# Zeroing a new batch's first column on VectorE, and reading the weighted sums behind the mask of the slot

## The chip, the cores and the metric

The kernel runs on one core of a Trainium2 chip. The metric is the device time of one execution in microseconds (us); the median of several runs is compared.

## What is computed

The reference is an attention that keeps only the 32 largest scores of each query, followed by a channel mix with a token shift. Shapes: 8 batches, 8 heads, 576 tokens, 64 columns per head; model width 512, hidden width 1024.

```python
scores = scale * np.matmul(q, k.transpose(0, 1, 3, 2))
kth = np.partition(scores, -top_k, axis=-1)[..., -top_k:-top_k + 1]
scores = np.where(scores >= kth, scores, -1000000000.0)
attn = np.exp(scores - np.max(scores, axis=-1, keepdims=True))
attn = attn / (np.sum(attn, axis=-1, keepdims=True) + 1e-09)
x = np.matmul(attn, v)                      # then (B, S, H * D)
x_prev = np.concatenate([np.zeros((B, 1, D)), x[:, :-1, :]], axis=1)
xk = mu_k * x + (1.0 - mu_k) * x_prev
xr = mu_r * x + (1.0 - mu_r) * x_prev
k = np.maximum(xk @ w_k, 0.0)
out = 1.0 / (1.0 + np.exp(-(xr @ w_r))) * (k * k @ w_v)
```

The first token of a batch has no token before it, so `x_prev` begins with a column of zeros.

## The kernel before

The attention is cut into 288 tiles of 128 queries. Two heads are worked on together; for each batch the program visits four pairs of heads with tiles 0 to 3 and then the same four pairs with tiles 4 to 8. The program is a pipeline of slots, written out in Python: in slot n the loop in `pipeline` issues one step each for several tiles that stand at different stages, in the order that the list `ORDER` (line 42) gives. Nothing reorders it afterwards; every engine runs its own instructions in exactly this order and waits on semaphores.

The steps that matter here, with the tile that each serves in slot n:

- `score` (tile n, L234 and L238): TensorE multiplies queries and keys into the PSUM tile `ps`.
- `keep` (tile n, L243): ScalarE copies `ps` to `sc` in SBUF.
- `c0` to `c6`, `best`, `drop`, `bounds` (tiles n-1 and n-2, L267 to L279): VectorE picks the largest scores of each piece of a row.
- `count` (tile n-2, L283) on ScalarE and `below` (L286) on GpSimd; `eighth` (L914) and `thr` (L291) on VectorE then find the threshold of tile n-3.
- `exp` (tile n-3, L294): ScalarE writes the exponentials into the PSUM tile `se`, of which there is one. `mask` (tile n-3, L297): VectorE multiplies `se` by the comparison with the threshold and writes `E`; its time includes a short reading of the row's sum.
- `turn` (tile n-4, L313): TensorE transposes `E`, ScalarE copies the result out as `et` (L314).
- `weigh` (tile n-5, L371 and L373): TensorE multiplies the transposed weights with the values.
- `place` (tile n-6, L379 or L384, in 96 of the slots, where a group of four tiles or the last single one is complete): VectorE multiplies these weighted sums by the inverse row sums `ri` and writes them to `xT`, the transposed rows of the batch. This is what the title calls reading the weighted sums; below it is the **place**.

The scores and the weighted sums lie in the same PSUM tile, side by side in the same two banks:

```python
scored = p("psS", 1, space=PSUM).tile([128, 2, 512], F32, name="ps")
g.ps = scored[:, :, :HS]
g.sums = scored[:, :, HS:HS + 128], scored[:, 0, HS + 128:HS + 192]
```

So the program has the next `score` on TensorE wait until the place has read the sums, and the place wait until `keep` has read the scores.

The channel mix runs in the same slots. Chunks of up to 256 tokens of finished rows are mixed (L403, L408, L413), split into a high and a low part (L427, L428) and multiplied with the weights (L432 to L434). This work comes in queues by engine (`L.soft`), from which a slot takes as much as a budget allows. `xT` has two buffers, one for each of two batches. Therefore, when the first place of a batch comes and the batch is the third or a later one, `L.force(g.read)` first issues all queued work up to the last reading of the rows, whatever the budget. Then `new_batch` takes the buffer and sets its first column to zero, 4 elements on each of 128 partitions (L690), on GpSimd. This happens eight times, at the first place of each batch. In the first 230 us VectorE, ScalarE and GpSimd also turn the weights of the channel mix, which come as 64-bit numbers, into pairs of 32-bit ones (L122 to L147).

Of the kernel before, what the change touches and what calls it, by code (L numbers as in the profile page):

```python
# [38 lines left out]
PACE, SHARE, PIECE, CAP, MOST = 4.60, 0.74, 1.52, 4.45, 2  # L39
END, HASTE = 36, 1.20  # L40
EXPS, EVAC = 3, (0, 'et')
ORDER = """exp norm score turn prep inv loads evac keep weigh sign best0 c0 drop0 c1 best1 c2 drop1 first c3 best2 c4 bounds eighth count et high below act late c5 norm2 early thr c6 second place mix mask dve pool weights""".split()


@with_exitstack
def topk_attention_channel_mix(ctx: ExitStack, tc: tile.TileContext, q, k, v, mu_k, mu_r, w_k, w_v, w_r, out):
    nc = tc.nc
# [639 lines left out]

    def new_batch(g):
        x = g.two.tile([128, HP, 1 + S], F32, name="xT")
        nc.gpsimd.memset(x[:, :, 0:1], 0.0)  # L690
        return x

    def pipeline(g):
# [91 lines left out]
        while n < total + 7 or "next" in state or L.busy():  # L785
# [96 lines left out]
            def ranks_(f, r):  # L882
                if C:
                    f(C, r)
# [40 lines left out]
            def place_():  # L925
                T = tiles.get(n - 6)
                if T and ends(T):
                    U = T.U
                    if U.P.b not in xT:
                        if state["start"] < (U.P.b - 1) * S:  # L930
                            save()
                        if U.P.b > 1:
                            L.force(g.read)
                        xT[U.P.b] = new_batch(g)
                    U.xT = xT[U.P.b]
                    place(U)
                    if U.P.hp == HP - 1 and T.i == U.P.part[-1]:
                        state["tokens"] = U.P.b * S + (S if T.i == 8 else 256)
                if V and V.i == V.P.part[-1] and V.P.hp == HP - 1:
                    o = slice(V.P.first, V.i + 1)  # L940
                    nc.vector.tensor_reduce(least[:, V.P.n // HP:V.P.n // HP + 1], V.P.group[:, :, 1:, o], axis=mybir.AxisListType.XYZ, op=OP.min)
# [5 lines left out]
            do.update({f"drop{r}": lambda r=r: ranks_(drop, r) for r in range(2)})  # L947
            for step in ORDER:
                if step in do:
# [24 lines left out]
    with tc.If(again > 0):  # L974
        with tc.For_i(0, B, 1) as b, ExitStack() as stack:
            g = Env()
            open_pools(stack, g, "_again")
            L = Direct()
            xT = new_batch(g)
            rows = out[bass.ds(b, 1)].rearrange("o s d -> (o s) d")  # L980
            for hp in range(HP):
# [56 lines left out]
```

## Time and profile before

| what | us |
|---|---|
| median of 3 runs (lowest, highest) | 1448.99 (1447.81, 1449.4) |
| the profiled execution | 1450.08 |
| its span, from the first to the last instruction | 1448.2 |

The profile is of one execution. Its trace says of every instruction when it began, how long it took, how long its engine stood idle before it and which instruction of another engine ended that idle time. "PE" is TensorE's matmuls, "PEld" its weight loads, "DVE" VectorE, "ACT" ScalarE, "POOL" GpSimd. A name such as `xT<-ps,ri` gives the tile written and the tiles read. The chain of waits is followed back from the last instruction to what released it at each step.

### The profile page before, as it was taken

Reading aid. Unit: us, or ns where it says so; the run is one execution under the profiler, and the core shown is the slowest. Engines: PE = TensorE matmul, PEld = TensorE weight load, DVE = VectorE, ACT = ScalarE, POOL = GpSimd, SP = SyncE. Lnnn points to the kernel's source line nnn. Section 1 sums busy time; section 2 is a strip of 40 time slices with the busy share of each in tenths; the row PEclk is TensorE's granted clock in tenths of the full one; section 3 lists DMA queues with packets and bytes.
Section 4 is the critical chain, followed back from the end, with each engine's and each line's share of the span. In section 5 each row is a group of like instructions: output and inputs, shape, how many; then the busy total and the mean of one; then the engine's idle time right before and its main releaser. Section 6 shows DMA issues by size and latency. Waiting matters only on the chain.

```text
span 1448.2 us, 32903 instructions
## 1 busy us (share of the span) xinstructions
PE 1289.6 (89%) x9909; PEld 971.8 (67%) x9909; DVE 1205.7 (83%) x6454; ACT 1160.8 (80%) x2662; POOL 968.2 (67%) x876
## 2 busy tenths in 40 slices
PE   5657767999989999898989999999999998999997
PEld 3444555676867676675767687777767676777786
DVE  6999899888888888888888988888888897889610
ACT  5677777898879888878879899888888887888741
POOL 3658886576656865656758776776676765667683
PEclk9886888999999999999999999999999999899999
DMA  4332232222121222112121222212221222111000
GB/s 98 82 91 75 55 88 70 57 48 57 45 64 39 59 60 60 41 44 62 44 60 40 52 59 57 47 50 62 54 58 41 49 64 65 33 45 42 20 16 21
DMA packets 243817, 78.79 MB, mean 54 GB/s; under 512 B 236464, under 2 KB 236464, under 8 KB 243632
## 3 DMA queue, kind: packets, MB, share of 16 engines
q1 hardware_dynamic: 243632, 76.61, 21.9%
q8 instruction: 82, 1.34, 0.4%
q14 instruction: 103, 0.84, 0.2%
HBM read 67.11 MB, written 9.44 MB: 53 GB/s over the span
## 4 chain that ended last, share of the span: by engine, by line
PE 59%; DVE 19%; ACT 13%; POOL 5%; issue 2%; DMA 1%; SPq 0%; ACTq 0%; DVEq 0%; POOLq 0%
PE ps L371 8%; PE ps L234 8%; PE pt L313 6%; PE ph L432 5%; PE ph L433 4%; PE ph L434 4%; PE pv L432 4%; PE pv L434 4%; PE pv L433 4%; DVE cand L267 3%; DVE E L297 3%; ACT sc L243 3%; ACT sg L283 2%; DVE top L914 2%; ACT xm L408 2%
## 5 line engine op out<-in xcount | busy, mean ns | idle before, releaser
L286 POOL TENSOR_TENSOR sg<-sc,sg 128x576 f32<-128x576 f32 x288 | 420.8, 1461 | 410.3 <-ACT sg L283 363.7
L267 DVE MAX8 cand<-sc 128x8 f32<-128x82 f32 (+1 forms) x2016 | 465.9, 231 | 4.5 <-ACT sc L243 3.7
L243 ACT ACTIVATE sc<-ps 128x576 f32<-128x576 f32 x288 | 186.3, 647 | 128.1 <-PE ps L234 104.6
L234 PE MATMUL ps<-K,qs 64*128 64x288 f32 x1024 | 206.4, 482 | 57.8 <-DVE xT L379 42.6
L283 ACT ACTIVATE sg<-sc,seen 128x576 f32<-128x576 f32 x288 | 222.1, 771 | 44.3 <-DVE seen L278 40.5
L914 DVE MAX8 top<-sg 128x8 f32<-128x576 f32 x288 | 216.6, 752 | 33.4 <-POOL sg L286 32.6
L297 DVE SCALAR_TENSOR_TENSOR E<-sc,seen,se 128x576 f32<-128x576 f32 x288 | 232.7, 808 | 0.9 <-DVE cand L267 0.6
L294 ACT ACTIVATE se<-sc,seen 128x576 f32<-128x576 f32 x288 | 213.8, 742 | 24.1 <-DVE E L297 23.7
L313 PEld LDWEIGHTS pt<-ident,E 128*128 128x128 f32 x1152 | 127.1, 146 | 152.6 <-issue 101.0
L313 PE MATMUL pt<-ident,E 128*128 128x128 f32 x1152 | 197.5, 297 | 32.6 <-DVE E L297 29.2
L371 PE MATMUL ps<-et,v_in 128*64 128x128 f32 (+1 forms) x2560 | 178.5, 286 | 27.4 <-ACT sc L243 26.4
L432 PE MATMUL ph<-xh,wk 128*128 128x256 f32 (+2 forms) x608 | 180.2, 296 | 1.1 <-ACT r L449 0.9
L371 PEld LDWEIGHTS ps<-et,v_in 128*64 128x64 f32 x2560 | 140.2, 147 | 59.6 <-ACT sc L243 51.6
L433 PE MATMUL ph<-xl,wk 128*128 128x256 f32 (+2 forms) x608 | 172.7, 284 | 8.3 <-POOL xl L428 8.3
L270 DVE MAX8 top<-cand 128x8 f32<-128x56 f32 x864 | 176.1, 204 | 0.1
L434 PE MATMUL ph<-xh,wk 128*128 128x256 f32 (+2 forms) x608 | 171.3, 282 | 0.0
L314 ACT ACTIVATE et<-pt 128x512 f32<-128x512 f32 x288 | 168.6, 585 | 1.5 <-PE pt L313 1.5
L234 PEld LDWEIGHTS ps<-K,qs 64*128 64x128 f32 x1024 | 81.9, 196 | 126.4 <-DVE xT L379 45.9
L432 PE MATMUL pv<-wv,hh 128*128 128x512 f32 (+1 forms) x296 | 126.3, 427 | 0.1
L433 PEld LDWEIGHTS ph<-xl,wk 128*128 128x128 f32 x608 | 116.6, 192 | 10.7 <-POOL xl L428 10.5
L432 PEld LDWEIGHTS ph<-xh,wk 128*128 128x128 f32 x608 | 116.4, 191 | 9.9 <-issue 6.2
L434 PE MATMUL pv<-wv,hl 128*128 128x512 f32 (+1 forms) x296 | 118.2, 399 | 2.8 <-POOL hl L453 2.7
(99 smaller groups left out, 2858.0 us busy)
## 6 DMA issues: line engine op xcount, KB each, us to landing
kt<-in_k SPq DMA_DIRECT2D x256, 72.0 KB, 2.3
q_near<-in_q SPq DMA_DIRECT2D x256, 64.0 KB, 2.2
v_in<-in_v SPq DMA_DIRECT2D x128, 128.0 KB, 2.5
out<-eb SPq DMA_DIRECT2D x35, 256.0 KB, 2.2
wst<-in_moe_w_k SPq DMA_DIRECT2D x8, 512.0 KB, 4.1
wst<-in_moe_w_v SPq DMA_DIRECT2D x8, 512.0 KB, 3.8
vr_in<-in_v SPq DMA_DIRECT2D x64, 32.0 KB, 2.4
wst<-in_moe_w_r SPq DMA_DIRECT2D x4, 512.0 KB, 4.0
```

Source lines behind the costliest of these rows:

```text
L234: nc.tensor.matmul(g.ps[:, e], lhsT=P.qs[j][h, c * 128:(c + 1) * 128], rhs=P.K[h, j], start=True, stop=True)
L243: nc.scalar.activation(T.sc.rearrange("p (e k) -> p e k", e=2), T.ps, AF.Copy)
L267: nc.vector.max(T.cand[:, 8 * i:8 * i + 8], T.sc[:, CUTS[i]:CUTS[i + 1]])
L283: nc.scalar.activation(T.side, T.sc, AF.Sign, bias=T.under, scale=-BELOW, accum_out=T.cnt)
L286: nc.gpsimd.tensor_mul(T.side, T.sc, T.side)
L297: nc.vector.scalar_tensor_tensor(T.e, T.sc, T.thr, g.pe, op0=OP.is_ge, op1=OP.mult, accum_out=T.rs)
L313: nc.tensor.transpose(pt[:, c, :], T.e[:, c * 128:(c + 1) * 128], ident)
L371: nc.tensor.matmul(pa[hs[j]], lhsT=P.v[:, j, c, :], rhs=ms[c][j], start=(c == 0), stop=False)
L432: nc.tensor.matmul(ps, lhsT=sh, rhs=mh, start=first, stop=False)
L433: nc.tensor.matmul(ps, lhsT=sh, rhs=ml, start=False, stop=False)
L434: nc.tensor.matmul(ps, lhsT=sl, rhs=mh, start=False, stop=last)
L914: nc.vector.max(M.top[:, 24:32], M.side)
```

## The change

Two things change. The memset of a new batch's first column goes from GpSimd to VectorE. And in `ORDER` the step `mask` stands ahead of `place`, which leaves `place` as VectorE's last step of the slot, ahead of the queued work only.

```diff
-ORDER = """... second place mix mask dve pool weights""".split()
+ORDER = """... second mask place mix dve pool weights""".split()
...
     def new_batch(g):
         x = g.two.tile([128, HP, 1 + S], F32, name="xT")
-        nc.gpsimd.memset(x[:, :, 0:1], 0.0)
+        nc.vector.memset(x[:, :, 0:1], 0.0)
         return x
```

The first place of a batch, on VectorE (the difference between the two orders; `nine` is the threshold, `E` the mask, `cand` and `top` belong to the next slot):

```order
 L291 SCALAR_TENSOR_TENSOR nine,seen<-se,cnt,top 128x9
 L267 MAX cand<-sc 128x8
-L379 TENSOR_TENSOR xT<-ps,ri 128x256
-L297 SCALAR_TENSOR_TENSOR E,rs<-sc,seen,se 128x576
+L297 SCALAR_TENSOR_TENSOR E,rs<-sc,seen,se 128x576
+L690 MEMSET xT 128x4
+L379 TENSOR_TENSOR xT<-ps,ri 128x256
 L270 MAX top<-cand 128x8
 L267 MAX cand<-sc 128x8
```

The place has moved behind the mask, and the memset stands between them, on the engine that runs both.

The same point of the program on GpSimd, in a batch where queued work was issued first (`xm` is the mixing's last reading of the rows, `sg` the step `below`):

```order
 L286 TENSOR_TENSOR sg<-sc,sg 128x576
 L413 TENSOR_TENSOR xm<-xm,xT 128x512 x2
-L690 MEMSET xT 128x4
 L286 TENSOR_TENSOR sg<-sc,sg 128x576
 L428 TENSOR_TENSOR xl<-xm,xh 128x512 x2
```

The memset is gone from its place behind the additions; nothing else moves on GpSimd.

An ordinary place, on VectorE; the other 88 are like it:

```order
 L291 SCALAR_TENSOR_TENSOR nine,seen<-se,cnt,top 128x9
 L267 MAX cand<-sc 128x8
-L379 TENSOR_TENSOR xT<-ps,ri 128x256
-L297 SCALAR_TENSOR_TENSOR E,rs<-sc,seen,se 128x576
+L297 SCALAR_TENSOR_TENSOR E,rs<-sc,seen,se 128x576
+L379 TENSOR_TENSOR xT<-ps,ri 128x256
 L270 MAX top<-cand 128x8
 L267 MAX cand<-sc 128x8
```

Mask and place have changed places. The orders of TensorE and ScalarE are the same before and after.

## Rows read from the trace of the kernel before

**Rows 1.** The page, busy time of each engine, share of the span, instructions.

```profile
PE 1289.6 (89%) x9909; PEld 971.8 (67%) x9909; DVE 1205.7 (83%) x6454; ACT 1160.8 (80%) x2662; POOL 968.2 (67%) x876
```

**Rows 2.** The page, chain that ended last, share of the span by engine.

```profile
PE 59%; DVE 19%; ACT 13%; POOL 5%; issue 2%; DMA 1%; SPq 0%; ACTq 0%; DVEq 0%; POOLq 0%
```

**Rows 3.** The place L379: what ended VectorE's idle time before it (us, times).

```profile
  PE ps L373: 48.8, 29
  POOL xT L690: 18.9, 7
  ACT sc L243: 13.8, 18
```

**Rows 4.** TensorE's waits for a place (us in total, times, longest).

```profile
PE ps L234 <- DVE xT L379: 42.6, 14, 5.9
PE ps L234 <- DVE xT L384: 7.2, 5, 3.2
```

**Rows 5.** The memset on GpSimd (ns: least, median, most; first and last start).

```profile
L690 POOL MEMSET xT<- x8: 95/106/112, 54.7 to 1228.7; 128x4 f32 x8
```

**Rows 6.** Timeline at the fourth batch's start, VectorE (start us, us, instruction, idle before).

```profile
581.23 0.42 DVE L379 TENSOR_TENSOR xT<-ps,ri 128x256 f32<-128x256 f32 x1 [3.98 <-POOL xT L690]
581.58 0.80 DVE L297 SCALAR_TENSOR_TENSOR E<-sc,seen,se 128x576 f32<-128x576 f32 x1
```

**Rows 7.** The same stretch, GpSimd.

```profile
578.84 2.31 POOL L413 TENSOR_TENSOR xm<-xm,xT 128x512 f32<-128x512 f32 x2 [0.33 <-ACT xm L408]
581.10 0.10 POOL L690 MEMSET xT<- 128x4 f32 x1
```

**Rows 8.** The same stretch, TensorE and ScalarE.

```profile
581.72 1.33 PE L234 MATMUL ps<-K,qs 64*128 64x288 f32 x4 [5.63 <-DVE xT L379]
582.42 0.75 ACT L294 ACTIVATE se<-sc,seen 128x576 f32<-128x576 f32 x1 [2.86 <-DVE E L297]
```

**Rows 9.** Timeline at the other seven batch starts, the engine that limits each.

```profile
54.84 0.43 DVE L379 TENSOR_TENSOR xT<-ps,ri 128x256 f32<-128x256 f32 x1 [1.24 <-POOL xT L690]
259.99 0.42 DVE L379 TENSOR_TENSOR xT<-ps,ri 128x256 f32<-128x256 f32 x1 [1.40 <-POOL xT L690]
421.66 0.76 PE L234 MATMUL ps<-K,qs 64*128 64x288 f32 x4 [1.10 <-DVE xT L379]
423.73 1.09 PE L371 MATMUL ps<-et,v_in 128*64 128x128 f32 x16 [0.41 <-ACT sc L243]
746.32 0.74 ACT L294 ACTIVATE se<-sc,seen 128x576 f32<-128x576 f32 x1 [2.85 <-DVE E L297]
909.48 1.09 PE L371 MATMUL ps<-et,v_in 128*64 128x128 f32 x16 [0.76 <-ACT sc L243]
1068.51 0.76 PE L234 MATMUL ps<-K,qs 64*128 64x288 f32 x4 [0.89 <-DVE xT L379]
1070.59 1.09 PE L371 MATMUL ps<-et,v_in 128*64 128x128 f32 x16 [0.41 <-ACT sc L243]
1228.89 0.43 DVE L379 TENSOR_TENSOR xT<-ps,ri 128x256 f32<-128x256 f32 x1 [2.32 <-ACT xh L427]
```

**Rows 10.** Busy time by stretch behind the fourth stall (us, five engines, clock, DMA).

```profile
581.70:586.20 4.50, 4.48 (x26) 3.40 (x28) 4.50 (x27) 3.65 (x8) 1.31 (x1) 0.50 0.11 26
```

**Rows 11.** The chain from 652 to 657 us (start us, us, what).

```profile
652.20 0.43 DVE xT L379
652.63 0.73 DVE E L297 x2
...
655.42 0.05 DVE seen L278
```

**Rows 12.** Timeline at one ordinary place, VectorE and then TensorE.

```profile
557.78 0.43 DVE L379 TENSOR_TENSOR xT<-ps,ri 128x256 f32<-128x256 f32 x1 [2.14 <-PE ps L373]
559.19 0.76 PE L234 MATMUL ps<-K,qs 64*128 64x288 f32 x4
```

**Rows 13.** Timeline behind the place at 240.79 us, TensorE.

```profile
241.05 0.78 PE L234 MATMUL ps<-K,qs 64*128 64x288 f32 x4 [3.24 <-DVE xT L384]
```

More of the change, by code (lines that the diff above doesn't have):

```diff
@@ L41 @@
 EXPS, EVAC = 3, (0, 'et')
-ORDER = """exp norm score turn prep inv loads evac keep weigh sign best0 c0 drop0 c1 best1 c2 drop1 first c3 best2 c4 bounds eighth count et high below act late c5 norm2 early thr c6 second place mix mask dve pool weights""".split()
+ORDER = """exp norm score turn prep inv loads evac keep weigh sign best0 c0 drop0 c1 best1 c2 drop1 first c3 best2 c4 bounds eighth count et high below act late c5 norm2 early thr c6 second mask place mix dve pool weights""".split()
 @with_exitstack
```

## The prediction

> **What bounds the kernel now.** I read the busy times first. TensorE is busy 89% of the span, VectorE 83%, ScalarE 80% [rows 1], so no engine has much room, and a stall that stops all of them is worth its full length. Then the chain that ended last: 59% TensorE, 19% VectorE, 13% ScalarE, 5% GpSimd [rows 2]. Up to some 240 us it runs mostly through VectorE, which converts the weights there; from then on mostly through TensorE. Next the waits around the place, because both halves of the change touch it. VectorE stands idle before L379 in 54 of 64 cases by three releasers: 29 times for the weighted sums (48.8 us), 18 times for the copy of the scores (13.8 us), 7 times for the memset (18.9 us) [rows 3]. The other way round, TensorE's scores wait for a place only 19 times, 42.6 and 7.2 us together [rows 4].
>
> Last, the timeline at the start of a batch. The memset takes 0.106 us [rows 5], but it stands in GpSimd's line behind work that was forced out before it. At the fourth batch the additions L413 run from 578.84 to 581.15 us and the memset follows at 581.10 [rows 7]. The place begins at 581.23 after VectorE has waited 3.98 us [rows 6]; TensorE's next score begins at 581.72 after 5.63 us, and ScalarE's next exponential, which needs the mask behind the place, after 2.86 us [rows 8]. So here three engines stand still for 0.1 us of work.
>
> **The change, part 1: the eight batch starts.** The wait for GpSimd goes. The memset now follows the mask on its own engine. What it costs on VectorE no row shows; below stands the 128x1 operation L278, which takes 0.05 us of the chain [rows 11], above the 0.106 us on GpSimd [rows 5]. I take 0.1, since it writes as many elements as GpSimd does. The mask needs neither memset nor sums, so it starts when VectorE arrives, and takes 0.73 us until the next instruction [rows 11]. The place then ends earlier than before by the old wait less 0.8 us (0.73 and 0.1, rounded); VectorE as a whole is earlier by the old wait less 0.1; ScalarE gets its mask at once and is earlier by its own idle time.
>
> What the kernel gains is what the engine gains that has least to gain and is loaded afterwards. Fourth batch: VectorE 3.98 - 0.1 = 3.9, TensorE 3.98 - 0.8 = 3.2 (of 5.63), ScalarE 2.86 [rows 6, 8]. I take 2.9. The fifth has the same shape, ScalarE's 2.85 [rows 9]: 2.9. In the first two VectorE limits: 1.24 - 0.1 = 1.1 and 1.40 - 0.1 = 1.3. In the third, sixth and seventh TensorE had other work during most of VectorE's wait, and only its own idle time can be won: 1.10 + 0.41 = 1.5; 0.76, so 0.8; 0.89 + 0.41 = 1.3. In the eighth the idle time is put down to ScalarE's L427, but the last memset starts at 1228.7 [rows 5] and ends as the place begins at 1228.89, so this is the memset again; TensorE waits for the place there, and gains 2.32 - 0.8 = 1.5 [rows 9]. Sum: 1.1 + 1.3 + 1.5 + 2.9 + 2.9 + 0.8 + 1.3 + 1.5 = **13.3 us**.
>
> What is late next: ScalarE's exponential, then the copy of the scores, for which L371 waits. Taking 0.1 us off GpSimd eight times is worth nothing; that engine is busy 67% [rows 1].
>
> **Part 2: the other 88 places, the good side.** Where VectorE waits ahead of a place, the mask now fills the wait, up to 0.73 us. With a wait of 2.14 us for the sums, as at 557.78 [rows 12], the place begins no later than before, since TensorE's sums set it, and VectorE is 0.73 us ahead afterwards. For most places that is worth nothing, because TensorE is the bound there and does not wait. In seven places, of which the one at 652.20 is shown, the chain goes through an ordinary place that had waited and on to the mask [rows 11]. There 0.73 us can be won, 5.1 us in all; the bounds are 0 and 5.1. I take half, 2.5 us, as the next chain is never far behind.
>
> **Part 3: the bad side.** Where VectorE did not wait ahead of the place, the place now comes 0.73 us later, and so does TensorE's next score if it was waiting. At 240.79 TensorE waited 3.24 us for it [rows 13], with the chain running from the place to the scores. That costs 0.73, rounded up to 0.8. Of the other 18 waits [rows 4], by their times, six are at batch starts and seven in the first 240 us, where TensorE has room; five are left. The bounds are 0.8 and 6 x 0.8 = 4.8; I take 0.8, since the chain runs through few of the five and the mask fits into a wait of VectorE's ahead of two. After an ordinary place TensorE has about one us of other work: the place at 557.78 ends at 558.21, and the next score begins at 559.19, 0.98 later, without waiting [rows 12]. That covers the 0.73; if that cover were gone, each place would cost up to 0.73.
>
> Two smaller moves cost nothing: the narrow place L384 moves like L379, and the reduction of row bounds L941 at the end of a visit moves behind the mask, with no one waiting for it before the very end.
>
> **The sum.** -13.3 - 2.5 + 0.8 = -15.0 us against the profiled execution's 1450.08: 1435.1. The median of the runs lies 1.1 us below that execution, so the time is **1434 us**.
>
> **The rivals.**
>
> *More than the sum.* After the long stalls TensorE runs slowly: behind the fourth the granted clock is 0.50, the 1.2 GHz level, for 4.5 us in which it is all but fully busy [rows 10]. A stall of 5.63 us becomes one of 2.5; if the clock does not fall then, 2.25 us come back in each of the fourth, fifth and eighth batch, 6.7 in all. With all of part 2 (2.6 more) that is 24.3 us, 1425. Against it speaks that ScalarE limits two of these starts. Chance 0.15.
>
> *The next wait takes the place.* The forced work still lies on ScalarE and GpSimd, whoever clears the column. If VectorE meets it a slot later, in L914 behind L286, only the starts without a long backlog keep their gain: 1.1 + 1.3 + 1.5 + 0.8 + 1.3 = 6.0, so 1443. Against it: GpSimd's next L286 depends on ScalarE, which waits for VectorE's mask. Chance 0.10.
>
> *It doesn't do what it says.* The new column's buffer was read by GpSimd's L403 and L413 two batches earlier. If VectorE's memset had to wait for the forced additions, the wait would stay and only parts 2 and 3 would be left, 2.5 - 0.8 = 1.7: 1447. The old memset was issued right behind those additions, but they read a later batch's rows or a saved copy. Chance 0.06, with whatever else ends in no change.
>
> *Slower: TensorE pays at each place.* Scores and sums share PSUM banks, so a later reading of the sums holds back the next scores. The trace shows the coupling: the place at 581.23 ends at 581.65, and the waiting score starts at 581.72 [rows 6, 8]. Each place that TensorE then waits for costs 0.73 us, and the turning point is 13.3 / 0.73 = 18 places. TensorE, no longer held up at batch starts, could catch up with VectorE at the 29 places that follow its own sums, and at 13 that it waits for now: 42 x 0.73 = 30.7, less 13.3, is 17 us slower, 1466 by the median. Against it: TensorE's work is the longest, and a faster start of a batch also brings VectorE forward. Chance 0.07.
>
> The Trainium skill has the rule behind this rival ("PSUM — Partial Sum Buffer", section "PSUM bank collisions raise a hardware error"): no two engines may access the same bank and quadrant at a time, reads included, so one must be made to wait for the other even where their columns are disjoint. By that rule alone every place would push the next score back by the mask's length, and 88 x 0.73 less 13.3 would be 51 us slower; the trace agrees that they wait for each other, but shows TensorE held up in only 19 of 96 places.
>
> **How the numbers follow.** My forecast, a gain between some 8 and 22 us, has the remaining chance, 0.62. Its low end is the batch starts with nothing from part 2 and all of part 3 against it, 13.3 - 4.8 = 8.5, 1440.5 by the median; its other end nears the first rival's 1425. The range reaches to that rival, 1424, and up to 1442, close to the second. About 0.2% (2.9 us) is what a measurement can tell from no change. Faster by more: 0.62 + 0.15 + 0.10 = 0.87; within: 0.06; slower: 0.07.
>
> **What would show it.** In the profile after: no place waits for L690; TensorE's waits for L379 fall from 42.6 us by some 10 at the batch starts (0.4 + 1.1 + 3.2 + 3.2 + 0.9 + 1.5); ScalarE's 2.86 and 2.85 us waits for the mask are gone; VectorE's idle time for the sums falls by up to 29 x 0.73 = 21 us. Part 1 is wrong if VectorE or ScalarE stands idle as long one slot later. Part 3 is wrong if TensorE's waits for the places grow in number far beyond 19, above all between 300 and 1350 us.

## The result and the profile after

| | median us (lowest to highest) | ratio to before, 95% interval |
|---|---|---|
| before | 1449.20 (1447.81 to 1449.96) | |
| changed | 1429.22 (1428.13 to 1429.90) | 0.9863 (0.9845 to 0.988) |

The kernel became 20.0 us faster; the forecast was 15, in a range from 7 to 25. The profiled execution took 1428.13 us, 21.95 less than the one of before, so parts read from the two traces add up to some 2 us more than the medians differ by.

The page after, busy time by engine and two of its costliest groups (idle time before the group and its releaser at the end of a line):

```profile
PE 1290.7 (90%) x9909; PEld 972.9 (68%) x9909; DVE 1208.0 (85%) x6462; ACT 1154.7 (81%) x2662; POOL 965.5 (68%) x868
...
L914 DVE MAX8 top<-sg 128x8 f32<-128x576 f32 x288 | 217.2, 754 | 45.9 <-POOL sg L286 44.3
...
L294 ACT ACTIVATE se<-sc,seen 128x576 f32<-128x576 f32 x288 | 213.5, 741 | 2.0 <-DVE E L297 1.8
```

The same two groups on the page of before:

```profile
L294 ACT ACTIVATE se<-sc,seen 128x576 f32<-128x576 f32 x288 | 213.8, 742 | 24.1 <-DVE E L297 23.7
...
L914 DVE MAX8 top<-sg 128x8 f32<-128x576 f32 x288 | 216.6, 752 | 33.4 <-POOL sg L286 32.6
```

The engines do the same work as before [rows 1]; what went is waiting. ScalarE waited 23.7 us for the mask and waits 1.8. VectorE, which is earlier now, waits 12 us more for GpSimd's product in L914.

The place and the memset after (what ended VectorE's idle time ahead of L379: us, times; then the memset in ns, as in [rows 5]):

```profile
  PE ps L373: 29.6, 29
  ACT sc L243: 2.0, 8
...
L690 DVE MEMSET xT<- x8: 62/62/62, 53.9 to 1207.9; 128x4 f32 x8
```

Against [rows 3] the 18.9 us for the memset are gone, the waits for the copy of the scores fell from 13.8 to 2.0, and the 29 waits for TensorE's sums lost 19.2 us: 0.66 each, nearly all of the mask's 0.73. The memset takes 0.062 us on VectorE.

TensorE's waits for the place after:

```profile
PE ps L234 <- DVE xT L379: 34.2, 12, 5.8
...
PE ps L234 <- DVE xT L384: 6.7, 4, 3.1
```

They are 16 and 40.9 us, where [rows 4] had 19 and 49.8. The fourth batch start after, on VectorE, TensorE and ScalarE in turn:

```profile
570.07 0.80 DVE L297 SCALAR_TENSOR_TENSOR E<-sc,seen,se 128x576 f32<-128x576 f32 x1
570.79 0.08 DVE L297 DVE_READ_ACCUMULATOR E<-sc,seen,se 128x1 f32 x1
570.83 0.06 DVE L690 MEMSET xT<- 128x4 f32 x1
571.00 0.43 DVE L379 TENSOR_TENSOR xT<-ps,ri 128x256 f32<-128x256 f32 x1
```

```profile
571.48 0.76 PE L234 MATMUL ps<-K,qs 64*128 64x288 f32 x4 [2.49 <-DVE xT L379]
```

```profile
572.36 0.73 ACT L294 ACTIVATE se<-sc,seen 128x576 f32<-128x576 f32 x1
```

VectorE no longer stands idle there; TensorE's 5.63 us [rows 8] became 2.49, and ScalarE's 2.86 became nothing. TensorE's next L371, with the transposed weights, runs slowly:

```profile
573.72 1.97 PE L371 MATMUL ps<-et,v_in 128*64 128x128 f32 x16 [0.24 <-ACT sc L243]
```

Where the time came from can be read from the start of ScalarE's copy of the scores (L243), which happens once for each of the 288 tiles: how much earlier it is than before, tile by tile. The table takes the difference between tile 14 and tile 8 of each batch as the gain of its start (the first place lies between them), and all else together as the rest; all from profiled executions, in us.

| kernel | eight starts, first to eighth | sum | rest |
|---|---|---|---|
| forecast | 1.1, 1.3, 1.5, 2.9, 2.9, 0.8, 1.3, 1.5 | 13.3 | 1.7 |
| changed | 0.4, 1.0, 2.7, 3.5, 3.0, 0.8, 1.5, 1.4 | 14.4 | 7.4 |
| memset_only | 1.1, 0.7, 1.8, 1.8, 4.2, 0.7, 1.4, -0.1 | 11.7 | 1.7 |
| order_only | 0.0, 0.9, 0.0, -0.4, 0.2, 0.9, 0.5, -0.1 | 2.0 | 8.5 |

A part of the rest is not the program's: fill_starts, below, is the same program as the changed kernel up to its fourth batch start, and its profiled execution was 2.7 us later than that one at tile 64, 2.2 of it lost before tile 48. Between the third start and the fourth the two agree; behind the third start the changed kernel's rest is 4.4 us.

### The profile page after: what moved, and what is told of

It reads as the page before. It is cut to its first block, busy times and chain, and to the rows that moved or that the text cites. A ratio compares the mean times of both kernels' runs of the same rounds, so it can differ in the third digit from the quotient of the medians.

```text
span 1426.4 us, 32864 instructions
## 1 busy us (share of the span) xinstructions
PE 1290.7 (90%) x9909; PEld 972.9 (68%) x9909; DVE 1208.0 (85%) x6462; ACT 1154.7 (81%) x2662; POOL 965.5 (68%) x868
## 4 chain that ended last, share of the span: by engine, by line
PE 44%; ACT 6%; POOL 3%; DVE 3%; issue 1%; ACTq 0%; DVEq 0%; POOLq 0%
PE ps L371 6%; PE ps L234 5%; PE pt L313 5%; PE pv L432 4%; PE ph L432 4%; PE pv L434 3%; PE pv L433 3%; PE ph L433 3%; PE ph L434 3%; ACT sc L243 2%; PE pz L432 2%; PE pz L433 1%; PE pz L434 1%; PE ps L373 1%; POOL sg L286 1%
## 5 line engine op out<-in xcount | busy, mean ns | idle before, releaser
L243 ACT ACTIVATE sc<-ps 128x576 f32<-128x576 f32 x288 | 186.5, 648 | 146.8 <-PE ps L234 101.9
L914 DVE MAX8 top<-sg 128x8 f32<-128x576 f32 x288 | 217.2, 754 | 45.9 <-POOL sg L286 44.3
L371 PE MATMUL ps<-et,v_in 128*64 128x128 f32 (+1 forms) x2560 | 179.0, 287 | 23.9 <-ACT sc L243 22.8
L371 PEld LDWEIGHTS ps<-et,v_in 128*64 128x64 f32 x2560 | 140.8, 147 | 55.3 <-ACT sc L243 44.5
```

Of the source, the lines that this page charges most:

```text
L243: nc.scalar.activation(T.sc.rearrange("p (e k) -> p e k", e=2), T.ps, AF.Copy)
L371: nc.tensor.matmul(pa[hs[j]], lhsT=P.v[:, j, c, :], rhs=ms[c][j], start=(c == 0), stop=False)
L914: nc.vector.max(M.top[:, 24:32], M.side)
```

## The experiments

All timings are beside runs of the kernel before on the same chip, whose medians were 1448.9 to 1449.7.

**memset_only: the first half alone**

```diff
-        nc.gpsimd.memset(x[:, :, 0:1], 0.0)
+        nc.vector.memset(x[:, :, 0:1], 0.0)
```

> The memset on VectorE, the place ahead of the mask as before. Theory 1 (the parts add up, and part 1 was sized about right): the eight batch starts give 13 to 14 us, so about 1435.5, and the other 6 us of the change's 20.0 belong to the order. Rival (part 2 was sized right and the batch starts undersized, by the clock that no longer falls): about 1431, 18 us. TensorE's longest waits for L379 of 5.6 us fall to about 1.8 here, since the place is not behind the mask.

1434.59 us (1433.79 to 1436.9), ratio 0.99 (0.9884 to 0.9915): a gain of 14.3. Theory 1 holds for the sum: the memset alone gives about what part 1 forecast. TensorE's longest wait for L379 stayed in the first 240 us; at the fourth start it is 1.76 us, as expected:

```profile
574.20 0.76 PE L234 MATMUL ps<-K,qs 64*128 64x288 f32 x4 [1.76 <-DVE xT L379]
575.02 0.63 PE L313 MATMUL pt<-ident,E 128*128 128x128 f32 x4
575.48 0.38 PE L203 MATMUL pq<-ident,q_near 128*128 128x128 f32 x2
577.16 1.98 PE L371 MATMUL ps<-et,v_in 128*64 128x128 f32 x16 [1.30 <-ACT sc L243]
578.93 0.64 PE L373 MATMUL ps<-el,vr_in 128*64 128x128 f32 x4
579.50 1.33 PE L234 MATMUL ps<-K,qs 64*128 64x288 f32 x4
```

TensorE starts earlier, then waits again, 1.30 us for ScalarE, and runs slowly from there on: the score at 579.50 takes 1.33 us where the one at 574.20 took 0.76. The granted clock of the two kernels behind this start, memset_only first, the changed kernel second (columns as in [rows 10]):

```profile
577.00:582.00 5.00, 4.83 (x30) 3.68 (x31) 5.00 (x31) 4.48 (x11) 4.40 (x4) 0.50 0.20 43
```

```profile
572.50:576.00 3.50, 3.26 (x27) 2.59 (x25) 3.19 (x19) 3.50 (x8) 3.06 (x4) 0.52 0.30 68
576.00:580.00 4.00, 4.00 (x25) 3.16 (x24) 4.00 (x28) 3.91 (x10) 4.00 (x4) 1.00 0.17 37
```

So here the earlier score won less: 1.8 us at this start against 3.5 with the mask ahead.

**order_only: the second half alone**

```diff
-ORDER = """... second place mix mask dve pool weights""".split()
+ORDER = """... second mask place mix dve pool weights""".split()
```

> The mask ahead of the place, the memset on GpSimd as before. Theory 1: the order was undersized; it gives about 6 us alone, 1443, more if ScalarE, which then gets its mask ahead of GpSimd's memset, wins at batch starts what TensorE still waits for. Rival (as predicted): 1.7 us, 1447.5, no change that can be told.

1439.46 us (1438.78 to 1440.66), ratio 0.9936 (0.9922 to 0.9949): 9.4 us faster, more than the 6 us of theory 1 and far more than the rival's 1.7. The waits ahead of L379:

```profile
  PE ps L373: 27.6, 28
  POOL xT L690: 15.3, 8
  ACT sc L243: 1.7, 7
```

The memset still holds up the place 8 times; the mask fills the other waits as in the changed kernel. By the table only 2.0 us of this gain lie at the batch starts; of the other 8.5, 2.5 lie ahead of the second start, where profiled executions of one program differ by some 2. The halves overlap: 14.3 + 9.4 is 23.7, the whole is 20.0.

**narrow_first, starts_first, mask_first_i7, mask_first_i3, mask_first_starts: the order by kinds of place**

In each, some places stand ahead of the mask as before, with VectorE's memset:

```diff
+            T6 = tiles.get(n - 6)
+            sums_first = bool(T6) and ends(T6) and (CONDITION)
             for step in ORDER:
-                if step in do:
+                if step == "mask" and sums_first:
+                    place_()
+                    mask_()
+                elif step == "place" and sums_first:
+                    pass
+                elif step in do:
                     do[step]()
```

with CONDITION `T6.i == 8` (narrow_first), `T6.i == 8 or T6.i == 3 and T6.P.hp == 0` (starts_first), `T6.i != 7` (mask_first_i7), `T6.i != 3` (mask_first_i3) and `not (T6.i == 3 and T6.P.hp == 0)` (mask_first_starts).

> The changed kernel, but the 32 narrow places L384 stand ahead of the mask as before. Theory 1: the gain of the order comes from the wide places, which had waited; a narrow place almost never waited, and TensorE waits for four of them, so each of the four comes 0.7 us earlier: 0 to 2.9 us faster than the changed kernel, 1426 to 1429. Rival (the early mask is worth something everywhere, by ScalarE's next exponential): slower than the changed kernel by 1 to 3 us, 1430 to 1432.

> As narrow_first, and the eight places at batch starts ahead of the mask too, behind VectorE's memset. If TensorE limits these starts now (it waits 2.5, 2.5 and 2.9 us for the place at the fourth, fifth and eighth), up to 0.7 us each is won against narrow_first: 2 us or more with the clock. If ScalarE limits them, nothing, or up to 2 us lost by its later mask.

> VectorE's memset; the mask goes ahead only at the 32 wide places of tiles 4 to 7, the ones that wait for TensorE's sums; the other 64 places stand ahead of the mask as before. Theory 1 (the order's gain comes from waits that the mask fills, and lies at these places): most of the 5.4 us between memset_only (1434.6) and the changed kernel (1429.2) come back, 1430 to 1432. Rival (the gain is spread over all places, by an earlier exponential on ScalarE): about a third, 1433.

> VectorE's memset; the mask goes ahead only at the 32 wide places of tiles 0 to 3, the eight batch starts among them; the other 64 stand ahead of the mask as before. Theory 1: these had shorter waits, for the copy of the scores, and the batch starts gain from a mask that is not held up: about 2 us against memset_only, 1432 to 1433. Rival (spread evenly): about 1433; with all of the gain at batch starts: 1429.

> VectorE's memset; the mask goes ahead at the eight batch starts alone, the other 88 places stand ahead of the mask as before. Against memset_only (1434.6) this asks what the early mask is worth at the starts. If the starts hold what starts_first lost against narrow_first: 2 us, 1432.5. If the order's gain needs the ordinary places too: no change, 1434.6.

| the mask goes ahead at | median us (lowest to highest) | ratio, 95% interval |
|---|---|---|
| no place (memset_only) | 1434.59 (1433.79 to 1436.9) | 0.99 (0.9884 to 0.9915) |
| the 32 of tiles 4 to 7 (mask_first_i7) | 1434.96 (1434.47 to 1435.78) | 0.9905 (0.9889 to 0.992) |
| the 32 of tiles 0 to 3 (mask_first_i3) | 1434.81 (1434.8 to 1435.72) | 0.9903 (0.9888 to 0.9918) |
| the 8 batch starts (mask_first_starts) | 1432.94 (1431.19 to 1433.8) | 0.9883 (0.9868 to 0.9898) |
| the 56 wide ones but the starts (starts_first) | 1434.06 (1432.37 to 1435.04) | 0.99 (0.9885 to 0.9915) |
| all 64 wide ones (narrow_first) | 1431.96 (1430.55 to 1432.29) | 0.9884 (0.9869 to 0.9899) |
| all 96 (changed) | 1429.22 (1428.13 to 1429.9) | 0.9863 (0.9845 to 0.988) |

The intervals reach some 2 us to either side, so neighbours in this table can't be told apart by their times alone; the traces say more. By the medians, the expectation that the gain lies at the tiles 4 to 7 fell: that third alone is no faster than none, and neither is the other wide third. Both wide thirds together win 2.6 us, and the narrow places, of which theory 1 said that they would lose 0 to 2.9, win another 2.7, as the rival said.

At the batch starts the traces agree with starts_first, which is 2.1 us slower than narrow_first, and with mask_first_starts, which is 1.7 us faster than memset_only and close to the 1432.5 expected. By the tiles' starts, the four kernels with the mask ahead there win 14.4 to 16.6 us (changed 14.4, mask_first_i3 14.5, narrow_first 15.6, mask_first_starts 16.6), the three with the place ahead 10.8 to 11.8 (starts_first 10.8, memset_only 11.7, mask_first_i7 11.8). The fourth start shows why, narrow_first first and starts_first second:

```profile
571.48 0.76 PE L234 MATMUL ps<-K,qs 64*128 64x288 f32 x4 [2.49 <-DVE xT L379]
573.71 1.97 PE L371 MATMUL ps<-et,v_in 128*64 128x128 f32 x16 [0.35 <-ACT sc L243]
```

```profile
571.37 0.76 PE L234 MATMUL ps<-K,qs 64*128 64x288 f32 x4 [1.76 <-DVE xT L379]
574.34 1.98 PE L371 MATMUL ps<-et,v_in 128*64 128x128 f32 x16 [1.12 <-ACT sc L243]
```

With the mask ahead, TensorE's score waits 0.73 us longer for the place. But then L371 waits 0.77 us less for ScalarE's copy of the scores: ScalarE limits this start, and TensorE stands idle for 2.8 or 2.9 us either way. Two tiles behind the start all seven kernels have won the same 3.0 us. The difference comes behind that, with the clock: in the four with the mask ahead it is at half for 3.4 us at this start, in the three with the place ahead for 6.8, and these win 1.8 to 2.1 us where the others win 3.5 to 3.7. At the fifth start memset_only's clock did not fall, and it wins 4.2.

At ordinary places behind the third start the gain comes in a few steps, each between one tile and one of the next few, and the same within 0.05 us in every kernel that has it, but for one. The table gives them in us, by the time in the kernel before; changed and order_only agree to 0.01:

| kernel | 815 | 1008 | 1107 | 1139 | 1316 |
|---|---|---|---|---|---|
| changed, order_only | 0.66 | 0.48 | 0.36 | 0.62 | 0.91 |
| narrow_first | 0.66 | 0.48 | 0.36 | -0.75 | 0.0 |
| starts_first | 0.65 | 0.47 | 0.34 | 0.60 | 0.0 |
| mask_first_i7 | 0.0 | 0.48 | 0.0 | 0.58 | 0.0 |
| mask_first_i3 | 0.0 | 0.0 | 0.36 | 0.0 | 0.0 |
| mask_first_starts, memset_only | 0.0 | 0.0 | 0.0 | 0.0 | 0.0 |

So the tiles 4 to 7 win at two places, the tiles 0 to 3 at one, one step needs both, and the narrow places win at one. That is why the wide thirds win more together than each alone. Between 650 and 696 us the kernels differ further, from a loss of 0.1 to a gain of 2.6 us; mask_first_i3 and narrow_first, which win least there, have one stretch of 6.8 us at half the clock in it, order_only, which wins most, one of 3.4.

The -0.75 of narrow_first is the clock. Around 1121 us narrow_first and the changed kernel run the same instructions on TensorE, with the same waits of 0.81 and 0.60 us ahead, and yet (changed first, narrow_first second):

```profile
1121.00:1125.00 4.00, 3.94 (x21) 2.76 (x22) 3.83 (x25) 3.65 (x11) 3.47 (x3) 1.00 0.45 100
```

```profile
1121.00:1125.00 4.00, 3.40 (x17) 2.44 (x14) 3.60 (x22) 3.94 (x12) 3.35 (x3) 0.64 0.36 78
```

The clock fell in the one and not in the other, and the next score on TensorE came at 1125.71 in the one and at 1127.70 in the other, where narrow_first had been only 0.66 us behind before. At the eighth start it is narrow_first that wins 0.9 us more (2.4 against 1.4). Over the whole run from 240 us on, TensorE's busy time times the missing share of the clock, summed over stretches of 4 us, comes to much the same in both, 17.3 and 17.0 us (19.6 in the kernel before), so the clock does not explain their difference as a whole.

**place_behind_queue: the place later still**

```diff
-ORDER = """... second mask place mix dve pool weights""".split()
+ORDER = """... second mask mix dve place pool weights""".split()
```

> The changed kernel, with the place another step later, behind VectorE's queued work of the slot (0 to 1.9 us of it). Theory 1 (TensorE has about one us after an ordinary place and waits for few): where the queue holds work, TensorE's score is late by that work less the slack; 2 to 8 us slower than 1429, and TensorE's waits for the place grow from 16 to over 20. Rival of the prediction (every later place costs its delay): more than 15 us slower.

1441.31 us (1439.13 to 1442.53), ratio 0.9944 (0.9931 to 0.9958): 12.1 us slower than the changed kernel, between the numbers of the two theories.

```profile
PE ps L234 <- DVE xT L379: 44.9, 14, 6.5
PE ps L371 <- ACT sc L243: 33.2, 34, 3.0
...
PE ps L234 <- DVE xT L384: 9.1, 6, 3.1
```

TensorE's waits for a place rise by 13 us, from 16 to 20 in number, and those of L371 for the copy of the scores from 22.8 to 33.2 us. But the whole rise of the first lies in the first 242 us (from 27.0 to 40.9); behind them these waits are 13.1 us here and 14.0 in the changed kernel. And at 245 us this kernel is only 3 us behind, so most of the loss comes later, some 5 us of it around the sixth batch start.

The edit also does more than move the place. The place counts the finished tokens, and `mix` begins a new chunk of the channel mix by that count; with the place behind `mix`, chunks can begin only a slot later, and TensorE's list of instructions differs from the changed kernel's at 6254 of 9909 positions, from 136 us on. So the 12.1 us can't be put down to the later place, and this run tests neither theory cleanly. That a later place holds back the score, the two orders at the fourth start show above: 0.73 us for 0.73.

**mask_before_c6: the mask earlier still**

```diff
-ORDER = """... early thr c6 second mask place mix dve pool weights""".split()
+ORDER = """... early thr mask c6 second place mix dve pool weights""".split()
```

> The changed kernel, with the mask one step earlier still, ahead of the last piece of the candidates (0.16 us) in every slot. If an early mask is worth something by ScalarE's exponential, up to 1 us faster, 1428; if VectorE's order is not what limits, no change, 1429.

1433.88 us (1433.6 to 1434.67), ratio 0.9898 (0.9882 to 0.9913): 4.7 us slower than the changed kernel. The mask's group on the two pages, changed first:

```profile
L297 DVE SCALAR_TENSOR_TENSOR E<-sc,seen,se 128x576 f32<-128x576 f32 x288 | 232.9, 809 | 0.6 <-PE px L323 0.3
```

```profile
L297 DVE SCALAR_TENSOR_TENSOR E<-sc,seen,se 128x576 f32<-128x576 f32 x288 | 234.5, 814 | 25.8 <-DVE nine L291 0.6 <-PE pt L313 0.5 <-PE ps L238 0.3
```

The mask reads the threshold that L291 has just written. Right behind it VectorE stands idle for 25.8 us in all, 0.09 each time in the mean; with the last piece of the candidates between them that time holds work. So the mask gains little from standing earlier, and the piece of candidates is pushed back. How this becomes 4.7 us is not shown: the loss is not spread evenly over the slots, and by the tiles' starts 3.6 us of it lie at the batch starts, which win 10.8 us here instead of 14.4.

**fill_starts: work for TensorE in the stalls that are left**

```diff
                 else:
                     L.run(step)
+            T6 = tiles.get(n - 6)
+            if T6 and T6.i == 3 and T6.P.hp == 0 and T6.P.b in (3, 4, 7):
+                fill = g.psM.tile([128, MAIN], F32, name="fill", tag="pm")
+                for _ in range(10):
+                    nc.tensor.matmul(fill, lhsT=wr[0][:, 0, :128], rhs=wr[0][:, 0, :], start=True, stop=True)
             L.end()
```

> The changed kernel, with ten extra matmuls of 128x512 (2.3 us by the rows of that form, results unused) on TensorE ahead of the score that waits for the place, at the fourth, fifth and eighth batch start, where TensorE now stands idle for 2.5 to 2.9 us and then runs at the 0.50 clock. Theory (the low clock behind these stalls costs time on the path): the clock stays at 1.00 there and up to 1.6 us come back at each, 1424.5 to 1428. Rival (ScalarE limits these starts, the clock costs nothing): no change, 1429. If the extra work is late it delays the score: 1429 to 1432.

1423.77 us (1423.04 to 1425.16), ratio 0.9821 (0.9808 to 0.9834): 5.4 us faster than the changed kernel, more than expected, by matmuls whose results nothing reads. TensorE at the fourth start, and the granted clock there:

```profile
571.43 2.57 PE L957 MATMUL fill<-wr 128*128 128x512 f32 x10
574.14 0.76 PE L234 MATMUL ps<-K,qs 64*128 64x288 f32 x4
574.83 0.66 PE L313 MATMUL pt<-ident,E 128*128 128x128 f32 x4
575.32 0.38 PE L203 MATMUL pq<-ident,q_near 128*128 128x128 f32 x2
576.37 1.09 PE L371 MATMUL ps<-et,v_in 128*64 128x128 f32 x16 [0.67 <-ACT sc L243]
```

```profile
573.00:575.00 2.00, 1.85 (x11) 0.94 (x10) 1.89 (x13) 2.00 (x6) 1.72 (x2) 1.00 0.79 227
575.00:577.00 2.00, 1.33 (x18) 1.09 (x19) 1.69 (x11) 2.00 (x6) 1.72 (x2) 1.00 0.48 107
```

The clock stays at 1.00; L371 takes 1.09 us instead of 1.97. By the tiles' starts the fourth, fifth and eighth batch win 4.3, 4.2 and 2.7 us against before, where the changed kernel wins 3.5, 3.0 and 1.4: 3.2 us more there. Another 1.5 us each come behind the fourth and the eighth start, where the changed kernel's clock falls once more, at 657.8 and at 1231.2 us, and this one's does not. Over the run from 240 us on the missing clock, summed as above, is 9.4 us instead of 17.3. This is the fastest kernel of the study.

## Why the prediction was right, and where it was off

**The range and the sign** held: 1429.22 lies between 1424 and 1442.

**What bounds the kernel** [rows 1, 2] held: all engines are as full as before, and a stall that stopped three of them paid in full.

**Part 1, the batch starts**, held, in its sum and mostly start by start: 14.4 us measured for 13.3. The rule behind it, that a start gains what the engine with least idle time gains, met the fifth to eighth start within 0.2 us. The third was undersized (2.7 for 1.5), because the sum stopped too early: behind the two waits of TensorE that it counts, 1.10 and 0.41 us, the trace of before has two more,

```profile
426.54 0.63 PE L313 MATMUL pt<-ident,E 128*128 128x128 f32 x4 [0.81 <-DVE top L270]
...
427.88 0.76 PE L234 MATMUL ps<-K,qs 64*128 64x288 f32 x4 [0.28 <-ACT sc L243]
```

and all four, 2.6 us, are gone in the changed kernel. The fourth was undersized too (3.5 for 2.9): 3.0 us come at the stall and 0.5 behind it, where the low clock lasts for 3.4 us instead of 6.8. In the first two the forecast was a little high. memset_only confirms that the sum is the memset's: 14.3 by the median, 11.7 at the starts. What the forecast did not say is that 2.7 of the 14.4 need the mask ahead, and that at the fourth start this is the clock. It did say that ScalarE is what is late next there, and narrow_first against starts_first shows it.

**Part 2, the other 88 places**, is the step that failed in size. It said: "I take half, 2.5 us, as the next chain is never far behind." With part 3 that made 1.7. Measured against the starts' 14.4, the rest is 20.0 - 14.4 = 5.6 us by the median; the trace has 4.4 us of it behind the third start, where the executions can be compared. The places were right in part. The chain of before passes through seven such places, at 176.91, 353.22, 652.20, 797.05, 816.77, 882.66 and 1139.27. The last wins 0.62 us, nearly the mask's 0.73; behind 652.20 the changed kernel wins 0.9, but there the clock differs too; 797.05 wins 0.10 at once, and the step of 0.66 at 815 follows; 353.22, 816.77 and 882.66 win nothing. The one at 176.91 can't be judged, since the first 240 us vary by 2 us from execution to execution. The steps at 1008, 1107 and 1316, 1.75 us together, come at places that the sum did not count, the last of them at a narrow place, which had no part in it. Why the step at 815 needs both wide kinds stays open.

**Part 3, the bad side**, was right about the one place that it priced. At 240.79 the next score lost 0.72 us: the tile before had come 3.75 us earlier than before the change, the score came 3.03 earlier. In narrow_first, where that place stands ahead of the mask, both came 3.6 earlier. The waits for the place, changed first:

```profile
238.02 1.33 PE L234 MATMUL ps<-K,qs 64*128 64x288 f32 x4 [3.05 <-DVE xT L384]
```

```profile
237.42 1.33 PE L234 MATMUL ps<-K,qs 64*128 64x288 f32 x4 [2.34 <-DVE xT L384]
```

This lies outside the starts, so the table has it in the rest. Behind the third start no tile of the changed kernel loses more than 0.2 us against the tile ahead of it, and TensorE's waits for the place fell in number, from 19 to 16.

**The rivals.** *More than the sum* was right about the price of the clock, but the change removes only part of it: a stall of 2.49 us is still followed by 0.52 for 3.5 us. It took fill_starts to get that back. *The next wait takes the place*: VectorE does wait 12 us more in L914, but spread over 87 waits of up to 0.8 us, and from the third on no start lost its gain. *It doesn't do what it says*: no place waits for L690 any more, and VectorE stands idle before none of the eight memsets. *Slower*: the coupling is real, 0.73 us more waiting at the fourth start and 0.72 us lost at 240.79, but it did not spread: TensorE's waits for a place went from 19 to 16, and those for L379 fell by 8.4 us, of some 10 forecast. By the Trainium skill's rule ("PSUM — Partial Sum Buffer", section "PSUM bank collisions raise a hardware error") scores and sums must take turns, since they share banks. The traces agree: the place at 571.00 ends at 571.43, and the waiting score starts at 571.48. A later place cost time by it only where TensorE was ready first.

## What to carry to other kernels

A tiny instruction costs what its queue costs: 0.1 us on GpSimd behind 2.3 us of forced additions stopped three engines at the fourth and fifth batch start, and on the engine that needs its result it took 0.062 us. When two instructions of one engine wait for different things, put the one that is ready first, but look at what the other one releases: 0.73 us of delay was free at the fourth batch start, where ScalarE was later still, and cost 0.72 us at the place at 240.79, where TensorE was on the path. When moving a step in such a program, see whether the order of the other engines stays the same: in place_behind_queue it did not. Where a stall on TensorE can't be removed, filling it with matmuls that nobody reads may pay, as it did here, where the time behind the stall ran at half the clock.

## What the runs showed of the hardware

- TensorE's granted clock fell to 0.5, the 1.2 GHz level, behind an idle time of 2.49 us at the fourth start; it did not with 2.57 us of matmuls in its place, and with such matmuls at three starts the kernel gained 5.4 us in all.
- The same two waits of 0.81 and 0.60 us were followed by a fall of the clock in one run and not in another, so small shifts elsewhere can cost or save more than a us at one place (1.3 us here).
- VectorE's mask right behind the instruction that writes its threshold stood idle 0.09 us each time in the mean, 25.8 us over 288 slots; with another instruction between them, 0.6 us.
